# A spectral mixer and a gated feed-forward on one core: how slab 0 is loaded, where four statistics rows are kept, and how the last slab is gated

## The chip, the core and the metric

The kernel runs on one core of a Trainium2 chip. The metric is the device time of one launch in microseconds; the number given for a kernel is the median of several runs. Profiles are of one execution, with times in microseconds from the start of its span. The engines are TensorE (PE; its weight loads are listed as PEld), VectorE (DVE), ScalarE (ACT), GpSimd (POOL) and SyncE (SP), which here only issues transfers.

## What is computed

A layer norm over the rows of `x` (2048 by 640) feeds two branches, which are multiplied and added to `x`:

```python
xn = _layernorm(x, axis=-1)
s = irfft2(rfft2(xn) * (w_r + 1j * w_i))          # over both axes, to bf16
g = silu((gelu(xn @ w_gate) * (xn @ w_up)) @ w_down)
return x + s * g
```

`w_gate` and `w_up` are 640 by 1536, `w_down` is 1536 by 640. Inputs, weights and output are bf16.

## The kernel before

The 2048 rows are taken as 16 slabs of 128 rows (row = 16 * n2 + n1, slab n1), each a tile of 128 partitions by 640. Both branches run through TensorE. The spectral branch is a chain of matrix products with tables (`fold`, `spectral`, `inverse`), with transfers to DRAM and back between its stages, and its result is the tile `y`. The feed-forward branch goes by four groups of four slabs: `gate_up` makes twelve tiles `uT` of a group (lines 868 to 920), and `down` multiplies them with `Wd` and finishes one slab (lines 932 to 1008).

No engine's order is written out by hand. Every piece of work is a task with an engine, a modelled cost, a rank and the tasks and buffers that it depends on (`add`, line 128). `Plan.run` (line 159) plays a list schedule with these costs and emits the instructions in the order that comes out; a load has either a modelled transfer time or, with `land=`, a fixed due time in nanoseconds. Each engine then works through its own queue in order. So a change of a cost, a due time or a buffer can change the order of tasks far away from it.

At the start, TensorE runs seven products on constants (`keep_warm`, line 377) while the first loads are on their way. Slab 0 of `x` is issued on ACT's DMA queue (line 349), slabs 1 and up and the weights on SP's (from line 372). For slabs 0 to 3, `turn_raw` (line 452) transposes the raw slab on TensorE in five pieces of 128 columns into PSUM (line 461), and a copy (`copy_on`, line 296) puts them into `XR`. The first two tiles of `gate_up` are made from `XR`, not yet normalised ("early", line 872); they are corrected later on VectorE with the mean and the inverse deviation of each row, spread over all partitions in `RB` (lines 916 and 918). These rows come from the statistics in `RM`: a transpose (line 560), a copy to a work tile `th` (line 562), a store of 4 KB to the DRAM scratch `D5` (line 563) and a load of `D5` into all partitions of `RB` (line 564). The work tiles tagged `th` have two buffers; the statistics on ACT (lines 416 and 419) and the tanh of `down` use the same tag.

At the end, the last slab (15) is done in three parts of 256, 256 and 128 columns (line 941). For each part twelve products (line 966) fill a PSUM tile, ACT takes tanh of half of it (line 975), and VectorE makes `G2 = (tanh + 1) * ps` (line 980), which is twice the silu; the factor of a half sits in the tables of the spectral branch. `finish` then multiplies by `y` (line 948), adds `x` (line 953) and stores. The third part goes another way: VectorE multiplies `y` with the PSUM tile beside the tanh (line 986, `early`), then applies `(tanh + 1)` (line 989, `late`), adds `x` (line 995), and the store is issued on ACT's queue (line 998).

Of the kernel before, what the change touches and what calls it, by code (L numbers as in the profile page):

```python
# [15 lines left out]
P = 128  # L16
# [206 lines left out]
def kernel(  # L223
# [125 lines left out]
    nc.scalar.dma_start(out=X[:, 0, :], in_=xv[:, 0, :])  # L349
# [21 lines left out]
    x_in[0] = add(lambda e: None, "SP", (1, 1), (0, -5), size=1, land=3620)  # L371
    load_x(1, 2, land=4150)
    load_w(Wg, gv, g_in, 0, 2, land=5210)
    load_x(2, 3, land=5700)
    load_w(Wu, uv, u_in, 0, 2, land=6760)
    load_x(3, 4, land=7250)
# [75 lines left out]
    def turn_raw(n1):  # L452
        pt = Slot("sp")

        def half():
            return pt.tile[:, 0, :].bitcast(BF16)[:, 0:D]

        def mm(e):
            place(pt, (2, 512))
            for c in range(5):  # L460
                nc.tensor.transpose(out=half()[:, c * P:c * P + P], in_=X[:, n1, c * P:c * P + P], identity=ident)  # L461
        a = add(mm, "PE", c_pe(*[140] * 5), (0, n1), after=[x_in[n1], warmed], new=[pt], use=[sX])
        raw[n1] = add(lambda e: copy_on(e, XR[:, :, n1 * P + (n1 > 0):(n1 + 1) * P + (n1 > 0)], half().rearrange("p (c n) -> p c n", c=5)),
                      {"ACT": c_act(640)} if n1 < 1 else {"ACT": c_act(640), "DVE": (415, 560)}, None, (0, n1), after=[a], use=[pt], hold={0: 1000, 1: 1000}.get(n1, 200))
# [92 lines left out]
    sr, rt = Slot("sp"), Slot("th")  # L557
# [4 lines left out]
    t = add(lambda e: nc.vector.tensor_copy(out=place(rt, (P,), FP32)[0:8, :], in_=sr.tile[0:8, 0, 0:P]), "DVE", c_dve(128, 1, True), (0, 3.5), after=[t], new=[rt], use=[sr])  # L562
    rs = dma(D5, lambda: rt.tile[0:8, :], (0, -5, 0), 4096, after=[t], use=[rt])
# [368 lines left out]
    def down(n1):  # L932
# [11 lines left out]
        def finish(lo, hi, done, rank, first):  # L944
            def f1(e):
                if first:
                    place(yg, (D,))
                (nc.gpsimd if n1 in () else nc.vector).tensor_tensor(out=yg.tile[:, lo:hi], in0=y.tile[:, n1 % 2, lo:hi], in1=G2.tile[:, lo:hi], op=ALU.mult)
# [10 lines left out]
        for lo, hi, tag in parts:  # L959
# [24 lines left out]
            def early(e, lo=lo, hi=hi, ps=ps, yp=yp):  # L984
                place(yp, (hi - lo,), FP32)
                nc.vector.tensor_tensor(out=yp.tile, in0=y.tile[:, n1 % 2, lo:hi], in1=ps.tile[:, 0:hi - lo], op=ALU.mult)
# [62 lines left out]
```

## Time and profile before

| | |
|---|---|
| median of 5 runs | 203.12 us (202.22 to 203.31) |
| the profiled execution | 202.22 us |
| its span | 200.4 us |
| granted TensorE clock | 0.999 |
| matmuls | 1526 |
| HBM read, written | 22.51 MB, 9.19 MB |

The profiled execution is the fastest of the five, and its span is what the profile's times are counted in. Busy times are of instructions on an engine; matmuls are pipelined with modelled ends, so a busy TensorE isn't the same as one at its peak. In a line of the timeline the numbers are the start and the length in us, then engine, line, operation, output <- input, shape and count; in brackets stands the idle time of the engine just before, and what ended it. A transfer's bracket or wait names the load that was waited for. "PEq", "ACTq" and the like are the engines' queues, where transfers are issued.

### The profile page before, as it was taken

Reading aid. Unit: us, or ns where it says so; the run is one execution under the profiler, and the core shown is the slowest. Engines: PE = TensorE matmul, PEld = TensorE weight load, DVE = VectorE, ACT = ScalarE, POOL = GpSimd, SP = SyncE. Lnnn points to the kernel's source line nnn. Section 1 sums busy time; section 2 is a strip of 40 time slices with the busy share of each in tenths; the row PEclk is TensorE's granted clock in tenths of the full one; section 3 lists DMA queues with packets and bytes.
Section 4 is the critical chain, followed back from the end, with each engine's and each line's share of the span. In section 5 each row is a group of like instructions: output and inputs, shape, how many; then the busy total and the mean of one; then the engine's idle time right before and its main releaser. Section 6 shows DMA issues by size and latency. Waiting matters only on the chain.

```text
span 200.4 us, 4122 instructions
## 1 busy us (share of the span) xinstructions
PE 195.2 (97%) x1526; PEld 117.8 (59%) x1526; DVE 148.8 (74%) x321; ACT 126.9 (63%) x224; POOL 31.6 (16%) x71
## 2 busy tenths in 40 slices
PE   8999999999999999999999999999999999999991
PEld 3994444676544555777755455467755555457781
DVE  1898889997333159999998999933257789787774
ACT  3999969966432767777775667243466665675421
POOL 2604250697000000000000000000004022211210
PEclk9999999999999999999999999999999999999999
DMA  6999999898539676533234110117604243332432
GB/s 180 327 316 326 337 395 212 219 253 163 183 106 377 225 189 179 134 110 112 64 111 136 65 65 0 69 65 237 286 3 144 89 134 108 101 101 85 131 103 65
DMA packets 35894, 32.62 MB, mean 163 GB/s; under 512 B 10910, under 2 KB 32930, under 8 KB 35874
## 3 DMA queue, kind: packets, MB, share of 16 engines
q1 hardware_dynamic: 34434, 29.49, 49.8%
q0 software_dynamic: 1152, 2.66, 4.8%
q8 instruction: 12, 0.20, 0.4%
q10 hardware_dynamic: 288, 0.20, 0.3%
q14 instruction: 8, 0.07, 0.1%
HBM read 22.51 MB, written 9.19 MB: 158 GB/s over the span
## 4 chain that ended last, share of the span: by engine, by line
PE 96%; DMA 2%; ACT 0%; DVE 0%; issue 0%; DVEq 0%
PE pg L882 26%; PE pu L882 26%; PE pg L966 13%; PE pu L966 13%; PE sp L693 3%; PE sp L826 3%; PE sp L768 2%; PE sp L802 2%; PE sp L666 2%; PE sp L528 2%; DMA X<-in_A_x_dram 2%; PE sp L686 1%; PE sp L820 1%; PE sp L461 1%; PE sp L474 1%; PE sp L649 0%
## 5 line engine op out<-in xcount | busy, mean ns | idle before, releaser
L882 PE MATMUL pg<-xnT,Wg 128*128 128x512 bf16 (+1 forms) x245 | 57.4, 366 | 0.0
L882 PE MATMUL pu<-xnT,Wu 128*128 128x512 bf16 (+1 forms) x245 | 57.3, 366 | 0.0
L903 DVE TENSOR_TENSOR uT<-pu,ge 128x512 bf16<-128x512 f32 x46 | 31.7, 690 | 20.0 <-PE pu L882 14.5
L966 PEld LDWEIGHTS <-uT 128*128 128x128 bf16 x396 | 37.8, 98 | 13.5
L899 ACT ACTIVATE ge<-pg 128x512 bf16<-128x512 f32 x46 | 27.5, 599 | 23.1 <-PE pg L882 22.6
L882 PEld LDWEIGHTS <-Wg 128*128 128x128 bf16 x285 | 25.3, 98 | 22.5 <-issue 0.4
L882 PEld LDWEIGHTS <-Wu 128*128 128x128 bf16 x285 | 24.9, 98 | 21.7
L966 PE MATMUL pg<-Wd,uT 128*128 128x320 bf16 (+2 forms) x204 | 30.7, 293 | 0.0
L966 PE MATMUL pu<-Wd,uT 128*128 128x320 bf16 (+1 forms) x192 | 29.7, 297 | 0.0
L296 ACT CAST ma<-sp 128x644 bf16<-128x644 f32 (+1 forms) x32 | 23.4, 794 | 9.7 <-PE sp L826 7.9
L928 POOL COPY xr<-s 1x1 bf16<-1x1 bf16 x1 | 0.2, 179 | 100.7 <-DVE s L852 100.7
L296 ACT CAST mc<-sp 128x640 bf16<-128x640 f32 x16 | 10.8, 697 | 5.5 <-DMA D<-mc 4.8
L975 ACT ACTIVATE th<-pu 128x320 f32<-128x320 f32 (+1 forms) x16 | 7.0, 437 | 11.0 <-PE pu L966 9.6
L929 POOL DMA_DIRECT2D xr<-in_A_x_dram x16 | 8.8, 550 | 32.3 <-DVE res L953 30.2
L980 DVE SCALAR_TENSOR_TENSOR G<-th,pg 128x320 bf16<-128x320 f32 (+1 forms) x16 | 7.7, 482 | 8.3 <-ACT th L975 8.1
L296 ACT CAST IU<-sp 128x640 bf16<-128x640 f32 x16 | 10.9, 691 | 4.1 <-PE sp L768 4.1
L296 ACT CAST Vt<-sp 128x640 bf16<-128x640 f32 x16 | 10.8, 691 | 3.7 <-PE sp L802 3.7
L975 ACT ACTIVATE th<-pg 128x320 f32<-128x320 f32 (+2 forms) x17 | 7.3, 430 | 8.2 <-PE pg L966 8.0
L980 DVE SCALAR_TENSOR_TENSOR G<-th,pu 128x320 bf16<-128x320 f32 (+1 forms) x16 | 7.7, 482 | 5.6 <-ACT th L975 5.3
L844 DVE TENSOR_TENSOR mb<-ma 128x640 bf16<-128x640 bf16 x8 | 3.9, 492 | 6.9 <-ACT ma L296 6.9
L409 DVE BATCH_NORM_STATS2 STAT<-X 128x6 f32<-128x320 bf16 x12 | 5.5, 484 | 4.0 <-DMA X<-in_A_x_dram 4.0
L746 DVE TENSOR_TENSOR R<-Y 64x644 bf16<-64x644 bf16 x16 | 7.8, 490 | 0.4
(104 smaller groups left out, 254.5 us busy)
## 6 DMA issues: line engine op xcount, KB each, us to landing
BU<-D SPq DMA_DIRECT2D x8, 640.0 KB
D<-mc SPq DMA_DIRECT2D x8, 320.0 KB
D<-IU SPq DMA_DIRECT2D x8, 320.0 KB
xr<-in_A_x_dram POOLq DMA_DIRECT2D x16, 160.0 KB, 2.6
out_dram<-res SPq DMA_DIRECT2D x15, 160.0 KB
Wg<-in_B_w_gate_dram SPq DMA_DIRECT2D x6, 320.0 KB
Wu<-in_B_w_up_dram SPq DMA_DIRECT2D x6, 320.0 KB
Wd<-in_B_w_down_dram SPq DMA_DIRECT2D x6, 320.0 KB
```

The source lines that it names most:

```text
L296: return nc.scalar.copy(out=out, in_=in_) if e == "ACT" else nc.vector.tensor_copy(out=out, in_=in_)
L409: nc.vector.bn_stats(out=STAT[:, n1, 6 * g:6 * g + 6], in_=x[:, 320 * g:320 * g + 320])
L693: nc.tensor.matmul(into(q, ri), lhsT=sZ.tile[:, q, ri, :], rhs=FM[:, kinds[q][2] + (4 if ri and kind == 0 else 0), :], start=False, stop=T ...
L746: nc.vector.tensor_tensor(out=o, in0=Yf[:, ::-3, :], in1=Yf[:, 1:3, :], op=ALU.subtract)
L826: nc.tensor.matmul(into(q, s), lhsT=svs[s].tile[:, c, :], rhs=IM[:, q, :], start=False, stop=True, skip_group_check=True)
L882: nc.tensor.matmul(ps.tile[:, lo:hi + more], lhsT=w[:, c, t * P:(t + 1) * P], rhs=XR[:, c, lo + (lo > 0):hi + 1 if lo or more else hi] if ...
L899: nc.scalar.activation(out=ge.tile, in_=pg.tile if src is None else src, func=ACT.Gelu_apprx_tanh)
L903: nc.vector.tensor_tensor(out=u.tile, in0=pu.tile if src is None else src, in1=ge.tile, op=ALU.mult)
L929: nc.gpsimd.dma_start(out=sx.tile, in_=xv[:, n1, :])
L966: nc.tensor.matmul(ps.tile[:, 0:hi - lo], lhsT=uT[grp, ks[i]].tile[:, j * P:(j + 1) * P], rhs=Wd[:, ks[i], lo:hi], start=(i == 0), stop=(i ...
L975: nc.scalar.activation(out=th.tile[:, 0:hi - lo], in_=ps.tile[:, 0:hi - lo], func=ACT.Tanh, scale=0.5)
L980: nc.vector.scalar_tensor_tensor(out=G2.tile[:, lo:hi], in0=th.tile[:, 0:hi - lo], scalar=1.0, in1=ps.tile[:, 0:hi - lo], op0=ALU.add, op1 ...
```

## The change

Four things are edited. Slab 0 is loaded by SP's queue as the first of its loads instead of by ACT's queue, and the due times of the loads are set anew. The transposes of slab 0 go in two steps of three and two pieces, into the two halves of the PSUM tile, each with a copy of its own on ACT. The statistics rows are copied into eight partitions of `RB` itself rather than into a `th` tile, and stored from there. For slab 15, ACT applies Silu in place of tanh, straight into `G2`, for all three parts; `finish` multiplies by `y` and by 2.0 in one VectorE instruction, and the third part goes through `finish` as well, with its store on ACT's queue as before. The modelled cost of the first Silu has 1300 ns added.

```diff
-    nc.scalar.dma_start(out=X[:, 0, :], in_=xv[:, 0, :])
...
-    x_in[0] = add(lambda e: None, "SP", (1, 1), (0, -5), size=1, land=3620)
-    load_x(1, 2, land=4150)
-    load_w(Wg, gv, g_in, 0, 2, land=5210)
-    load_x(2, 3, land=5700)
-    load_w(Wu, uv, u_in, 0, 2, land=6760)
-    load_x(3, 4, land=7250)
+    load_x(0, 1, land=3600)
+    load_x(1, 2, land=4050)
+    load_w(Wg, gv, g_in, 0, 2, land=5110)
+    load_x(2, 3, land=5600)
+    load_w(Wu, uv, u_in, 0, 2, land=6660)
+    load_x(3, 4, land=7150)
...
+        parts = ((0, 3), (3, 5)) if n1 < 1 else ((0, 5),)
+        for k, (lo, hi) in enumerate(parts):
+            def mm(e, k=k, lo=lo, hi=hi):
+                if k == 0:
+                    place(pt, (2, 512))
+                for c in range(lo, hi):
+                    nc.tensor.transpose(out=half(k)[:, c * P:c * P + P], in_=X[:, n1, c * P:c * P + P], identity=ident)
+
+            def cp(e, k=k, lo=lo, hi=hi):
+                copy_on(e, XR[:, lo:hi, n1 * P + (n1 > 0):(n1 + 1) * P + (n1 > 0)], half(k)[:, lo * P:hi * P].rearrange("p (c n) -> p c n", c=hi - lo))
...
-    t = add(lambda e: nc.vector.tensor_copy(out=place(rt, (P,), FP32)[0:8, :], in_=sr.tile[0:8, 0, 0:P]), "DVE", c_dve(128, 1, True), (0, 3.5), after=[t], new=[rt], use=[sr])
-    rs = dma(D5, lambda: rt.tile[0:8, :], (0, -5, 0), 4096, after=[t], use=[rt])
+    t = add(lambda e: nc.vector.tensor_copy(out=RB[0:8, 0, 0, :], in_=sr.tile[0:8, 0, 0:P]), "DVE", c_dve(128, 1, True), (0, 3.5), after=[t], use=[sr])
+    rs = dma(D5, RB[0:8, 0, 0, :], (0, -5, 0), 4096, after=[t])
...
+                if last:
+                    nc.vector.scalar_tensor_tensor(out=yg.tile[:, lo:hi], in0=y.tile[:, n1 % 2, lo:hi], scalar=2.0, in1=G2.tile[:, lo:hi], op0=ALU.mult, op1=ALU.mult)
+                    return
...
+            if last and hi == D:
+                add(lambda e: nc.scalar.dma_start(out=outv[:, n1, lo:], in_=res.tile[:, lo:]), "ACT", (430, 430), (0, 0, n1), after=[t], use=[res], size=256 * (hi - lo))
+                return
...
+            def gate(e, lo=lo, hi=hi, ps=ps):
+                if lo == 0:
+                    place(G2, (D,))
+                nc.scalar.activation(out=G2.tile[:, lo:hi], in_=ps.tile[:, 0:hi - lo], func=ACT.Silu)
+            if last:
+                a = add(gate, "ACT", c_act(hi - lo, extra=0 if lo else 1300), (0, step[0]), after=mm[-1:] + done, new=[] if lo else [G2], use=[ps, G2] if lo else [ps])
+                done.append(a)
+                finish(lo, hi, [a], (0, step[0]), lo == 0)
+                continue
```

With these go the lines of `early`, `late` and the branch for the third part (984 to 1002 before).

## The prediction, made before the changed kernel had run

> **What bounds the kernel now.** I read the page's totals first, then the windows, then TensorE's waits, the chain, and the timeline of both ends. The totals and the chain say TensorE:
>
> ```profile
> span 200.4 us, 4122 instructions
> PE 195.2 (97%) x1526; PEld 117.8 (59%) x1526; DVE 148.8 (74%) x321; ACT 126.9 (63%) x224; POOL 31.6 (16%) x71
> PE 96%; DMA 2%; ACT 0%; DVE 0%; issue 0%; DVEq 0%
> ```
>
> A busy share is an average, so the next two views ask where the missing 5.2 us lie: busy time by window, and everything that TensorE waited for.
>
> ```profile
> 4.00:8.00 4.00, 3.67 (x53) 3.51 (x54) 3.48 (x15) 3.17 (x6) 1.57 (x4) 1.00 1.08 311
> 8.00:12.00 4.00, 4.00 (x75) 4.00 (x73) 3.55 (x11) 3.55 (x8) 1.52 (x5) 1.00 1.13 332
> 196.00:200.40 4.40, 0.37 (x7) 0.20 (x4) 1.56 (x7) 0.40 (x2) 0.00 (x0) 0.95 0.23 74
> ...
> PE sp L367 <- PEq L1033: 0.8, 1, 0.8
> PE pg L882 <- ACT XR L296: 0.2, 1, 0.2
> PE sp L461 <- DMA X<-in_A_x_dram: 0.2, 1, 0.2
> ```
>
> The columns of a window are its length, then the busy time of PE, its loads, DVE, ACT and POOL. From 8 to 196 us PE is full in every window I asked for; it waits three times in all, and all three lie before 5.6 us. Its work is fixed, so the end moves by three things only: when the first product starts, what runs after the last product, and any new hole between. The first end:
>
> ```profile
> 4.08 1.25 PE L461 MATMUL sp<-ident,X 128*128 128x128 bf16 x10 [0.17 <-DMA X<-in_A_x_dram]
> 4.83 1.29 ACT L296 COPY XR<-sp 128x640 bf16<-128x640 bf16 x2 [2.17 <-PE sp L461]
> 5.57 0.73 PE L882 MATMUL pg<-XR,Wg 128*128 128x129 bf16 x10 [0.25 <-ACT XR L296]
> 7.41 0.49 DVE L409 BATCH_NORM_STATS2 STAT<-X 128x6 f32<-128x320 bf16 x1 [0.25 <-DMA X<-in_A_x_dram]
> 7.56 0.44 PE L461 MATMUL sp<-ident,X 128*128 128x128 bf16 x5
> ```
>
> Slab 0 lands at 4.03 (in the chain its DMA runs 0.72 to 4.03), five transposes and one copy follow, and the products start at 5.57. Slab 3 lands at about 7.4, where DVE waits for it, and PE reaches it at 7.56 without a wait: a lead of only 0.15. The other end:
>
> ```profile
> 195.74 0.39 ACT L975 ACTIVATE th<-pu 128x256 f32<-128x256 f32 x1 [0.93 <-PE pu L966]
> 196.41 0.28 ACT L975 ACTIVATE th<-pg 128x128 f32<-128x128 f32 x1 [0.28 <-PE pg L966]
> 196.72 0.29 DVE L986 TENSOR_TENSOR mc<-s,pg 128x128 f32<-128x128 bf16 x1
> 196.93 0.28 DVE L948 TENSOR_TENSOR yg<-s,G 128x256 bf16<-128x256 bf16 x1
> 197.13 0.28 DVE L989 SCALAR_TENSOR_TENSOR yg<-th,mc 128x128 bf16<-128x128 f32 x1
> 197.33 0.29 DVE L953 TENSOR_TENSOR res<-yg,xr 128x256 bf16<-128x256 bf16 x1
> 197.53 0.22 DVE L995 TENSOR_TENSOR res<-yg,xr 128x128 bf16<-128x128 bf16 x1
> 197.78 0.36 ACTq L998 DMA_DIRECT2D out_dram<-res  x1
> ```
>
> PE is done at 196.4. VectorE then works off five operations, two of them left over from the second part, and the last store leaves at 197.78; from there to the end is 2.62 us of transfer and closing.
>
> **What the Trainium skill says.** On the table: "ScalarE: Activation LUTs", What ACT_TABLE_LOAD costs, prices a switch of function set at 1283 ns of load plus about 1380 ns of drain. The trace agrees with the first (its one load takes 1.28 us); with the drain it doesn't visibly agree: the next ACTIVATE starts at 2.46, 0.02 after the load's end at 2.44. "ScalarE activation tables: per-element evaluation and per-set limits", What a function is on this engine, says that a function costs the same whichever table is read; so I give Silu the durations of tanh. No page says whether Silu shares a set with gelu and tanh. "DMA: Bandwidth & Descriptors", Issuing engines are not separate DMA queues, says that loads issued from several engines interleave on the same 16 DMA engines and only issue time is saved. The trace fits: from 2.6 us they move some 350 GB/s, and the share stays at 1.0 or more to 8 us.
>
> **The change, part by part.**
>
> *Slab 0 on SP.* Now slabs 0 and 1 are issued together at 0.72 on two queues and share the engines. Summing the windows of 0.2 us, the stream starts at 2.4, and the 0.33 MB of both have moved by 3.4; slab 0 lands 0.63 later, at 4.03. Alone in front, its 0.164 MB have moved by 2.92 and land at about 3.55. PE's seven warming products hold it to about 3.77 (0.76 + 7 x 0.43), so the transposes start there instead of at 4.08: 0.31 earlier. Every SP issue behind it comes one issue later, about 0.46 us (slab 1 from 0.72 to 1.18, Wg to 1.64, slab 3 from 2.68 to about 3.2). I cost that at nothing: slab 1 can begin at 2.4 + 0.46 = 2.86, just as slab 0 ends, and after that the transfers, not the issues, set the pace (slab 3's bytes move near 6 us). Without that cover it costs up to 0.46. On ACT's queue the 0.41 us issue ahead of the table load goes, which nobody waits for.
>
> *Two copies instead of one.* The transposes run 0.107 apart, so the third ends 0.21 before the fifth. A copy of 640 takes 0.70; at 0.83 ns per element (tanh: 0.28 at 128, 0.38 at 256) 384 take 0.49 and 256 take 0.38, and back-to-back copies overlap by 0.10. From the third transpose to the end: 0.04 + 0.49 - 0.10 + 0.38 = 0.81, against 0.21 + 0.04 + 0.70 = 0.95 now. Gain 0.14; ACT is charged 0.07 more. The first product can start at 5.57 - 0.31 - 0.14 = 5.12. The first columns of Wg allow that, barely: 0.656 MB have moved by 4.32, landing about 4.95.
>
> The 0.45 doesn't all last. The loads are no faster in sum, so slab 3 still lands near 7.4, and PE in its fixed order would reach it at 7.1 and wait. If it lands as now, only 0.10 is left (7.46 instead of 7.56); if it lands 0.1 earlier, as the due times in the diff assume, 0.20; if the new order puts other products ahead of it, up to 0.45. I take 0.25.
>
> *Rows in a corner of RB.* The same copy (0.27) and the same 4 KB store (issued at 17.04) as now. RB is filled only by the load that follows that store, so no wait is added. A "th" buffer comes free earlier, perhaps letting slab 7's statistics (L416, 20.54) run sooner on an ACT that is 85% busy there; PE isn't waiting: 0. The cover is PE's backlog; without it a late RB costs what it is late.
>
> *Silu and the gate.* For the last part go L986, L989 and their place in DVE's queue; for the first two, L980 (0.42 each). New: Silu in place of tanh, three scalar_tensor_tensor, the same adds. The trace shows no such operation on bf16 from SBUF at 256 columns; it lies between 0.29 (tensor_tensor, L948) and 0.42 (L980 from PSUM). I take 0.42, and 0.28 for 128 columns (L989). A dependent DVE step starts 0.03 after its source ends (195.50 + 0.29 to 195.82). Second part: Silu ends 196.13, gate 196.16 to 196.58, add 196.61 to 196.90. Last part: Silu 196.41 to 196.69, gate at 196.81 behind that add's issue (0.20 step) to 197.09, add 197.12 to 197.34, store at 197.37: 0.41 earlier. With the cheap gate the last gate starts at 196.72 and the store leaves at 197.2: 0.55.
>
> The table: if Silu is in another set, one load of 1.28 is due between the tanh of slab 14 (193.12 to 193.56) and the first Silu (194.43). If it needn't wait for PE it ends at 194.84, and the first Silu is 0.41 late, before two parts with slack: nothing lost. If it stands behind the wait for PE, it ends at 195.71; queued behind it are all three Silus, the third still at 196.41, but DVE's six steps then start at 196.1 and end near 197.6, a gain of 0.15. I take 0.48 for this part, between 0.41 and 0.55.
>
> *Sum:* 0.25 + 0.48 = 0.73. On the profiled execution: span 199.7, time 201.5 (1.82 lies around its span, 202.22 - 200.4). That execution is 0.90 below the median 203.12; from the median I get **202.39 us**.
>
> **Rivals.**
> A. Both ends gain as above: 202.39, own range 201.9 to 202.9. For it: the three waits and the five DVE steps are all at the ends. Chance 0.50.
> B. The gain is mostly eaten: slab 3's landing leaves 0.10 and the table load waits, leaving 0.15: 202.9. For it: the lead of 0.15 at 7.41. Against it: only one of the two need fail. Chance 0.22.
> C. Slower, by the plan: all instructions are ordered by a planner from modelled costs, and new due times and tasks reorder everything after 4 us. The order now has no hole in 190 us; the new one need not be so lucky. Place: a PE product put ahead of a transfer or an evacuation that comes later than modelled, most likely from 8 to 50 us, where DVE, ACT and DMA are near full. One such wait costs what the late thing is late; it decides from 0.73 + 0.6 = 1.3 us, and at 1.6 gives 203.12 - 0.73 + 1.6 = 204.0. Against it: the order of before has held 0.00 of waits there. Chance 0.20.
> D. The switch of set costs load and drain, 2.66, behind the wait at 194.43: first Silu at 197.1, last ends near 198.0, store near 198.5, 0.7 later than now; with 0.10 in front, 203.7. It decides from about 1.4, where the third Silu would move. Against it: no drain after the load at 1.16. Chance 0.08.
>
> **How the numbers follow.** This kernel's runs can tell about 0.3% (0.6 us) from no change: faster means under 202.5, slower over 203.7. A gives faster 0.41 and same 0.09; B faster 0.06, same 0.16; C slower 0.17, same 0.03; D slower 0.05, same 0.03. Faster 0.47, same 0.31, slower 0.22. The range takes A's lower end (0.45 + 0.55, and 0.3 for the draw of the median) and reaches past B and D into C until about 0.15 is left above: 201.8 to 203.9.
>
> **What would show it.** Slab 0 landing at 3.5 to 3.6 and the first L882 near 5.1; then whether L461 for slab 3 shows a wait on the load of X. A second ACT_TABLE_LOAD after 193.5, and whether it starts before PE's part is done. The last store at 197.2 to 197.4 less the front's gain. PE's list of waits: any entry after 8 us is C. Wrong is the reasoning if slab 0 lands no earlier, or if PE waits in the middle.

## The result, and the profile after

The changed kernel takes **203.97 us** (median of 31 runs, 202.81 to 204.9). The kernel before, run beside it 52 times, takes 202.62 (202.18 to 204.31); the five runs shown above had a median of 203.12. The ratio is 1.0054, 95% interval [1.0043, 1.0066]: the change makes the kernel slower by half a per cent. (The ratios and intervals are those recorded with the runs; they aren't quotients of the two medians, which would be 1.0067 here.) The forecast was 202.39 and faster. It was counted from the median of the first five runs; from 202.62 the same gain of 0.73 would give 201.89. Each experiment below is compared with the kernel before on its own chip; the medians of before lie between 202.51 and 202.65 there.

The page of the changed kernel (its profiled execution took 204.92 us, which is 0.95 above the median), first its totals and then the shares of the chain that ended last:

```profile
span 203.2 us, 4119 instructions
PE 194.8 (96%) x1526; PEld 117.4 (58%) x1526; DVE 147.3 (73%) x318; ACT 127.5 (63%) x226; POOL 30.8 (15%) x71
...
PE 92%; DMA 4%; ACT 1%; issue 0%; SPq 0%; DVE 0%; DVEq 0%; ACTq 0%
```

TensorE has the same 1526 matmuls and no more busy time (194.8 against 195.2); the span is 2.7 longer (203.15 against 200.44, before rounding). So the loss lies in waits, and the list of everything that TensorE waited for says in which (the numbers are us in total, times, longest):

```profile
PE pg L889 <- DMA Wg<-in_B_w_gate_dram: 1.9, 1, 1.9
PE sp L535 <- ACT mc L296: 1.7, 2, 1.5
PE sp L366 <- PEq L1034: 0.8, 1, 0.8
```

The last was there before. The first two are new, one at the start and one in the middle. The timeline of the start:

```profile
0.72 0.86 SPq L303 DMA_DIRECT2D X<-in_A_x_dram  x2
1.63 0.43 SPq L303 DMA_DIRECT2D Wg<-in_B_w_gate_dram  x1
...
3.71 0.74 PE L463 MATMUL sp<-ident,X 128*128 128x128 bf16 x10
...
6.31 0.74 PE L889 MATMUL pg<-XR,Wg 128*128 128x129 bf16 x10 [1.87 <-DMA Wg<-in_B_w_gate_dram]
...
8.23 0.49 DVE L408 BATCH_NORM_STATS2 STAT<-X 128x6 f32<-128x320 bf16 x1 [0.31 <-DMA X<-in_A_x_dram]
8.35 0.44 PE L463 MATMUL sp<-ident,X 128*128 128x128 bf16 x5
```

The transposes do start 0.37 earlier than before (3.71 against 4.08), but the first product starts 0.74 later (6.31 against 5.57), since the first columns of `Wg` are late, and slab 3, on which VectorE waits until 8.23, lands 0.8 later (7.41 before). TensorE reaches slab 3 at 8.35 instead of 7.56: 0.79 lost. The middle, the lines of SP's queue, ACT and PE around the wait:

```profile
42.93 5.00 SPq L499 DMA_TRANSPOSE xnT<-s  x3
48.02 0.54 SPq L303 DMA_DIRECT2D D<-mc  x1
51.37 1.29 ACT L296 CAST mc<-sp 128x640 bf16<-128x640 f32 x2 [3.31 <-DMA D<-mc]
52.11 0.38 PE L535 MATMUL sp<-mb,F1T 128*128 128x512 bf16 x1 [1.54 <-ACT mc L296]
```

Three transposing transfers stand in SP's queue ahead of a store of an `mc` tile. They take 5.0 us where three such issues of 1.23 would take 3.7; the store leaves at 48.02, ACT waits 3.31 us for it before it can write the next `mc` (there are two buffers), and TensorE waits 1.70 for ACT's copies. The end:

```profile
196.38 1.28 ACT L999 ACT_TABLE_LOAD   x1
197.67 0.38 ACT L999 ACTIVATE G<-pg 128x256 bf16<-128x256 f32 x1
...
199.21 0.28 ACT L999 ACTIVATE G<-pg 128x128 bf16<-128x128 f32 x1 [0.28 <-PE pg L979]
...
200.18 0.37 ACTq L968 DMA_DIRECT2D out_dram<-res  x1
```

TensorE's last matmul ends at 199.17 (198.34 + 0.83), and the last store leaves 1.01 us after it; before it was 1.41 (196.37 to 197.78). The end gains 0.40 up to that store. But the way from the last store to the end of the span is 0.30 longer (2.97 against 2.67, before rounding), so little of the gain is left. That isn't chance: it is 2.96 to 2.97 in all five profiles of kernels planned with the new due times, whichever queue loads slab 0, and 2.48 to 2.67 in the other fifteen. The last store lands 1.59 after its issue in both; a closing step on SP comes 0.33 later. Why isn't shown. So this execution's 2.7 us come from 0.79 at the start and 1.70 in the middle, less 0.40, plus 0.30 at the end; 0.3 are not located.

### The profile page after: what moved, and what is told of

Read it like the earlier page. It is cut to its first block, busy times and chain, and to the rows that moved or that the text cites. A ratio compares the mean times of both kernels' runs of the same rounds, so it can differ in the third digit from the quotient of the medians.

```text
span 203.2 us, 4119 instructions
## 1 busy us (share of the span) xinstructions
PE 194.8 (96%) x1526; PEld 117.4 (58%) x1526; DVE 147.3 (73%) x318; ACT 127.5 (63%) x226; POOL 30.8 (15%) x71
## 4 chain that ended last, share of the span: by engine, by line
PE 92%; DMA 4%; ACT 1%; issue 0%; SPq 0%; DVE 0%; DVEq 0%; ACTq 0%
PE pg L889 26%; PE pu L889 26%; PE pu L979 12%; PE pg L979 12%; PE sp L700 3%; PE sp L833 3%; PE sp L775 2%; DMA Wg<-in_B_w_gate_dram 2%; PE sp L809 2%; PE sp L673 2%; DMA D<-mc 2%; PE sp L535 1%; PE sp L693 1%; PE sp L827 1%; PE sp L481 1%
## 5 line engine op out<-in xcount | busy, mean ns | idle before, releaser
L906 ACT ACTIVATE ge<-pg 128x512 bf16<-128x512 f32 x46 | 28.0, 609 | 25.4 <-PE pg L889 25.3
L993 DVE SCALAR_TENSOR_TENSOR G<-th,pg 128x320 bf16<-128x320 f32 x15 | 7.3, 488 | 10.2 <-ACT th L988 9.9
L988 ACT ACTIVATE th<-pg 128x320 f32<-128x320 f32 x15 | 6.6, 440 | 10.4 <-PE pg L979 10.2
L993 DVE SCALAR_TENSOR_TENSOR G<-th,pu 128x320 bf16<-128x320 f32 x15 | 7.3, 487 | 6.1 <-ACT th L988 6.0
L988 ACT ACTIVATE th<-pu 128x320 f32<-128x320 f32 x15 | 6.7, 444 | 7.8 <-PE pu L979 6.6
L296 ACT CAST Z<-sp 128x1024 bf16<-128x1024 f32 x8 | 7.9, 1016 | 2.5 <-PE sp L673 2.5
L415 ACT ACTIVATE th<-X 128x640 bf16<-128x640 bf16 x10 | 7.7, 785 | 1.2 <-DMA X<-in_A_x_dram 1.2
```

Of the source, the lines that this page charges most:

```text
L296: return nc.scalar.copy(out=out, in_=in_) if e == "ACT" else nc.vector.tensor_copy(out=out, in_=in_)
L415: nc.scalar.activation(out=place(junk, (D,)), in_=x, func=ACT.Copy, scale=-1.0 / D, accum_out=less)
L906: nc.scalar.activation(out=ge.tile, in_=pg.tile if src is None else src, func=ACT.Gelu_apprx_tanh)
L988: nc.scalar.activation(out=th.tile[:, 0:hi - lo], in_=ps.tile[:, 0:hi - lo], func=ACT.Tanh, scale=0.5)
L993: nc.vector.scalar_tensor_tensor(out=G2.tile[:, lo:hi], in0=th.tile[:, 0:hi - lo], scalar=1.0, in1=ps.tile[:, 0:hi - lo], op0=ALU.add, op1 ...
```

## The experiments

Theory 1 after the result: moving slab 0 to SP's queue costs at the start, the new order costs in the middle, and the Silu gate gains what was forecast (up to the last store). Rivals: the table load or Silu costs more than it brings; the statistics rows in `RB` cost; the middle's wait follows from the transfers at the start and not from the order.

### The parts alone

**Silu alone**: `down` of the changed kernel in the kernel before; TensorE's order doesn't move (in short form).

```diff
-            th = tanh(...) ; G2 = (th + 1) * ps ; early / late for the third part
+            nc.scalar.activation(out=G2.tile[:, lo:hi], in_=ps.tile[:, 0:hi - lo], func=ACT.Silu)
+            finish(lo, hi, [a], (0, step[0]), lo == 0)
```

> Only the gate of slab 15 is changed; TensorE's order is that of before and slab 0 stays on ACT's queue. Theory 1 (the tail does what the forecast said, and what it saved in the changed kernel was lost behind its last store because that store was the first on ACT's queue): last store 0.4 us earlier after TensorE's end than before, 2.6 us from it to the end of the span, time 0.4 us less than before (ratio 0.998). Theory 2 (the table load or the extra ACT work costs something by itself): last store earlier but time the same or more. Theory 3 (the saved 0.4 is lost in the store whatever was on the queue earlier): 3.0 us from the store to the end, ratio 1.000.

Measured: 202.22, ratio 0.998 [0.9965, 0.9995]. Its timeline at the end:

```profile
193.65 1.28 ACT L992 ACT_TABLE_LOAD   x1
194.95 0.38 ACT L992 ACTIVATE G<-pg 128x256 bf16<-128x256 f32 x1
...
197.46 0.35 ACTq L961 DMA_DIRECT2D out_dram<-res  x1
```

The load stands directly before the first Silu and ends 0.02 ahead of it. The last store leaves 1.01 after TensorE's end (195.62 + 0.83), as in the changed kernel, and 0.32 earlier than before (197.78); 2.67 follow, as before. The end gains 0.2%. The expectation blamed the longer way behind the last store on that store being the first on ACT's queue; with slab 0 moved and nothing else (the next kernel) it is the first too, and the way is 2.51.

**Slab 0 on SP, nothing else**: one word of line 349; due times and the orders of all engines stay.

```diff
-    nc.scalar.dma_start(out=X[:, 0, :], in_=xv[:, 0, :])
+    nc.sync.dma_start(out=X[:, 0, :], in_=xv[:, 0, :])
```

> Only the issue of slab 0 moves from ACT's queue to the head of SP's; every engine's order stays that of before. Theory 1 (SP's issues for the weights come 0.46 us later while the first slabs start 0.4 us sooner, so the stream has a hole and all that follows lands later): slab 0 lands near 3.0, the first columns of Wg near 6.2, slab 3 near 8.2; TensorE reaches slab 3 about 0.8 us later than the 7.56 of before; time +0.6 to +0.9 us (ratio 1.003 to 1.0045). Theory 2 (the forecast: a stream without a hole): slab 3 lands at 7.4 and the time is 0.1 to 0.4 us less. Theory 3 (the new due times and the order made from them delay it): with the old order kept, no change at all.

Measured: 203.01, ratio 1.003 [1.0015, 1.0045]. The loss at the start needs nothing but the queue. TensorE's timeline:

```profile
5.66 1.26 PE L882 MATMUL pg<-XR,Wg 128*128 128x129 bf16 x10 [0.69 <-DMA Wg<-in_B_w_gate_dram]
...
7.25 1.27 PE L882 MATMUL pg<-XR,Wg 128*128 128x128 bf16 x10
```

Here is more than the wait of 0.69. Ten products of 128 columns take 1.27 us, and the next instruction starts 1.07 after them; before, ten took 0.73 and the next started 0.57 after (6.42 to 6.99). TensorE runs at half pace until 9.6 us in this execution (203.91 us, one of the slower ones; five of the 22 lie above 203.8).

**The rows in RB alone** (in short form):

```diff
-    ... out=place(rt, (P,), FP32)[0:8, :] ... ; rs = dma(D5, lambda: rt.tile[0:8, :], ...)
+    ... out=RB[0:8, 0, 0, :] ... ; rs = dma(D5, RB[0:8, 0, 0, :], (0, -5, 0), 4096, after=[t])
```

> Only the rows in a corner of RB instead of a th tile. TensorE's order becomes that of the changed kernel but for two products. Theory 1 (the freed th buffer reorders the plan, and this order has the wait for a copy of ma near 52 us behind the stores from mc): a TensorE wait on the mc copy of 0.5 to 1.8 us between 45 and 55 us, time +0.5 to +1.7 us (ratio 1.0025 to 1.008), with more spread than before. Theory 2 (the wait in the middle follows from the late loads at the start): no wait, time the same as before. Theory 3 (the forecast: the edit is free): the same time.

Measured: 202.39, ratio 0.9986 [0.9975, 0.9997]. TensorE's order becomes that of the changed kernel but for two products near 30 us, it has no wait in the middle, and it isn't slower. On SP's queue the `mc` store stays ahead of the third transposing transfer (44.39 and 45.02), as before.

**The split of slab 0's transposes alone** (the two-step loop of the change in `turn_raw`, the rest as before):

```diff
+        parts = ((0, 3), (3, 5)) if n1 < 1 else ((0, 5),)
```

> Only the two-step transposes and copies of slab 0; TensorE's order is that of before. Forecast: the first product starts 0.14 us earlier, and at most 0.10 of it is left behind slab 3: time 0 to 0.14 less, not told from no change (ratio 0.9993 to 1.000). Rival: the extra ACT instruction (0.07) pushes ACT, which is full from 5 to 10 us, and TensorE gains waits on XR: time +0.1 to +0.3.

Measured: 202.51, ratio 0.9991 [0.9975, 1.0007], not told from no change. The first product starts at 5.27 instead of 5.57; 0.09 of this is that the transposes began earlier in that execution (3.99 against 4.08), so the split brings 0.21.

**The loads alone**: slab 0 on SP with the new due times, so that the plan is made anew.

```diff
-    x_in[0] = add(lambda e: None, "SP", (1, 1), (0, -5), size=1, land=3620)
+    load_x(0, 1, land=3600)
```

> Only slab 0 on SP and the new due times, so the order is planned anew; gate, split and rows as before. With the old order this load cost 0.3%. Theory 1 (the due times, 0.1 us earlier while the loads really land 0.4 to 0.8 us later, make an order with waits): ratio 1.005 or more and waits of TensorE after 8 us. Theory 2 (the wait near 52 us needs the RB edit together with these due times): the same as with the old order, ratio 1.003, and no wait in the middle.

Measured: 203.19, ratio 1.0038 [1.0019, 1.0058], not told from the one-word edit. TensorE has no wait in the middle, and two transposing transfers, not three, stand ahead of the `mc` store on SP's queue. In the profiled execution (204.98 us) TensorE is at half pace until 10.2.

**All but the load**: the changed kernel with slab 0 on ACT's queue and the old due times; made twice, in two batches.

```diff
+    nc.scalar.dma_start(out=X[:, 0, :], in_=xv[:, 0, :])
-    load_x(0, 1, land=3600)
+    x_in[0] = add(lambda e: None, "SP", (1, 1), (0, -5), size=1, land=3620)
```

> The changed kernel with slab 0 back on ACT's queue and the old due times; the split, the rows in RB and the Silu gate stay. Theory 1 (the load on SP with its due times is the whole loss, at the start and through the order it makes): no wait of TensorE after 6 us, and the three gains add: ratio 0.998 x 0.9986 x 0.9991 = 0.9957, about 0.9 us less than before. Theory 2 (the edits hurt each other whatever the load does): a wait in the middle and a ratio over 0.999.

> The same as all_but_sp, whose interval (0.9967 to 1.0017) left open whether the three gains add. If they do, 0.9957 to 0.997; if not, 0.998 to 1.001 and a wait of TensorE that the other parts alone don't have.

Measured: 202.53, ratio 0.9992 [0.9967, 1.0017], and 202.31, ratio 0.9981 [0.9965, 0.9997]. The other three parts together are worth up to 0.2% (the first interval includes no gain), and the load with what it does to the plan turns that into a loss of 0.5%. The three single ratios would multiply to 0.9957: the gains don't add in full. In both profiles the `mc` store goes out ahead of the third transposing transfer. So the order of the changed kernel, with that store behind it, arises, in these runs, only when the new due times meet another of the edits.

**Silu and RB**: the two edits above in the kernel before.

> Before with the Silu gate and the rows in RB, and neither the load on SP nor the split. If the two gains (ratios 0.998 and 0.9986) add: 0.9966, about 0.7 us less than before. If all_but_sp's 0.9992 was right and the parts hurt each other: 0.998 to 1.000.

Measured: 202.17, ratio 0.9993 [0.9976, 1.0009]. The product of the two single ratios would be 0.9966, below that interval. In its profile TensorE waits 0.9 for the `mc` copies in the middle. Here the store (44.45) stands ahead of the held transposing transfer (45.07, 2.19 us), yet ACT can write the next `mc` only at 49.66, 5.2 us after the store's issue; in nine other profiles of this place it is 3.2 to 4.6. So the middle can wait for a store without the load on SP and without the order of the changed kernel. Why this store took so long isn't shown.

### The middle: the order or the early transfer?

**The changed kernel again**, as the control of its batch.

> The changed kernel once more, for a second trace beside the others. If the wait near 52 us belongs to its order, it is there again, with 0.5 to 1.8 us; if it was an accident of the first profile, TensorE waits only at the start, and the time of that profiled run is near 203.0. Ratio 1.003 to 1.007.

Measured: 203.93, ratio 1.0039 [1.0017, 1.0062]. The waits are 1.4 at the start and 1.2 in the middle; the third of the transposing transfers, issued at 44.48, is held 2.91, and the store leaves at 47.49.

**The changed kernel's orders with slab 0's transfer issued from ACT's queue**; due times and the order of every other instruction as in the changed kernel.

```diff
+    nc.scalar.dma_start(out=X[:, 0, :], in_=xv[:, 0, :])
-    load_x(0, 1, land=3600)
+    x_in[0] = add(lambda e: None, "SP", (430, 430), (0, -4, seq[0]), use=[sX], size=163840, land=3600)
```

> The changed kernel with every engine's order kept, and only slab 0's transfer issued from ACT's queue instead of SP's. Theory 1 (the hole at the start costs 0.6 to 0.9 us, the order in the middle costs the rest): slab 3 lands near 7.4 again, but a TensorE wait on the mc copy near 50 us stays; ratio about 0.999 to 1.002, and 0.6 to 0.9 us less than the changed kernel. Theory 2 (the wait in the middle is only the late start carried on): no wait after 6 us, ratio 0.996.

Measured: 202.72, ratio 1.0004 [0.9988, 1.0021]. SP's queue in the middle:

```profile
40.89 3.88 SPq L501 DMA_TRANSPOSE xnT<-s  x3
44.86 1.04 SPq L303 DMA_DIRECT2D D<-mc  x1
```

The same three transfers in the same order take 3.88. The third goes out at 43.54 and isn't held; in the two profiles of the changed kernel it goes out at 45.59 and 44.48, held 2.34 and 2.91. TensorE has no wait there. So this one edit of the changed kernel takes away its loss against before (1.0039 in the same batch), at the start and in the middle. The order alone isn't enough, then; it makes the place where a delay can do harm.

**The changed kernel with the store first**: one swap in SP's order, the third transposing transfer behind the store of `mc`. The orders of PE, ACT and DVE stay.

```diff
-        for t in plan.run():
+        line = plan.run()
+        at = line.index(stored[4])
+        back = [i for i in range(at) if line[i] in turns][-1]
+        line.insert(at, line.pop(back))
+        for t in line:
```

> The changed kernel with one swap on SP's queue: the fifth store from mc goes ahead of the transposing transfer that stood before it (issued at 44.48 and held for 2.91 us in the last trace); TensorE, VectorE and ACT keep their orders. Theory 1 (the wait in the middle is this store held behind that transfer, and the mc copy held behind the store): the store leaves near 45 instead of 47.5, ACT's wait for it falls from 2.8 to about 1 us, TensorE no longer waits on the mc copy near 51, and the time falls by about 1 us, to a ratio of 1.000 to 1.002. Theory 2 (the DMA engines are busy with the transposes then and the store would be as late anyway): TensorE's wait stays at 1 us or more, ratio 1.004 to 1.006.

Measured: 202.81, ratio 1.0022 [1.0005, 1.004]. The timeline of SP and ACT:

```profile
44.38 0.53 SPq L303 DMA_DIRECT2D D<-mc  x1
45.01 3.20 SPq L499 DMA_TRANSPOSE xnT<-s  x2
48.35 1.29 ACT L296 CAST mc<-sp 128x640 bf16<-128x640 f32 x2 [0.74 <-DMA D<-mc]
```

The transfer is held again, 45.01 onwards, but the store is out before it. ACT waits 0.74 instead of 3.31 and TensorE not at all; its list of waits shows only the two of the start:

```profile
PE sp L366 <- PEq L1040: 0.8, 1, 0.8
PE pg L889 <- DMA Wg<-in_B_w_gate_dram: 0.6, 1, 0.6
```

The swap takes the ratio from 1.0054 (1.0039 in the second batch) to 1.0022, in another batch: the middle costs some 0.2 to 0.3%, though the interval of the second batch alone overlaps. By the medians (203.97 and 203.93 to 202.81) it would be 1.1 us. That the wait is gone with the swap is shown by the list; its exact worth isn't, since this execution's wait for `Wg` is shorter too (0.6 against 1.9 and 1.4). What holds a transposing transfer issued near 45 us isn't shown; one issued at 44.81, in the kernel with the split alone, took 1.26. It is held in the kernel before too, where the store stands ahead of it:

```profile
43.20 1.22 SPq L492 DMA_TRANSPOSE xnT<-s  x1
44.51 0.53 SPq L303 DMA_DIRECT2D D<-mc  x1
45.10 1.82 SPq L492 DMA_TRANSPOSE xnT<-s  x1
```

### The start: why Wg is late, and what that costs

The windows of 0.4 us (columns: PE, loads, DVE, ACT, POOL, granted clock, DMA share, GB/s), with one of 1.2 us ahead of them, first of the kernel before, then of the changed one:

```profile
1.60:2.80 1.20, 1.20 (x4) 0.41 (x3) 0.00 (x0) 1.05 (x2) 0.24 (x4) 1.00 0.72 144
2.80:3.20 0.40, 0.40 (x2) 0.15 (x1) 0.00 (x0) 0.00 (x0) 0.00 (x0) 1.00 1.04 368
3.20:3.60 0.40, 0.40 (x2) 0.00 (x0) 0.00 (x0) 0.00 (x0) 0.00 (x0) 1.00 1.14 350
3.60:4.00 0.40, 0.31 (x1) 0.00 (x0) 0.00 (x0) 0.00 (x0) 0.00 (x0) 1.00 1.17 344
```

```profile
1.60:2.80 1.20, 1.20 (x4) 0.41 (x3) 0.00 (x0) 0.61 (x2) 0.24 (x4) 1.00 0.79 221
2.80:3.20 0.40, 0.40 (x2) 0.15 (x1) 0.19 (x1) 0.00 (x0) 0.00 (x0) 1.00 0.73 209
3.20:3.60 0.40, 0.40 (x2) 0.15 (x1) 0.40 (x2) 0.00 (x0) 0.00 (x0) 1.00 0.57 117
3.60:4.00 0.40, 0.40 (x6) 0.29 (x5) 0.36 (x2) 0.00 (x0) 0.00 (x0) 1.00 0.75 209
```

With both slabs on one queue in front, the stream has a hole from 2.8 to 4.0: (368 + 350 + 344 - 209 - 117 - 209) x 0.4 = 211 KB fewer moved. But it also picks up earlier, and (221 - 144) x 1.2 = 92 KB more have moved by 2.8. What is left behind at 4.0 is 119 KB, 0.34 us at 350 GB/s. Both slabs are there by 3.7 (ten transposes run through). The packet records of the two traces tell slabs and weights apart, since a row of a slab is a packet of 1280 bytes and a piece of `Wg` or `Wu` one of 512. The 256 packets of slabs 0 and 1 have started by 3.20 (before: 3.49). Packets of 512 bytes begin at 2.84, 1.2 us after `Wg` is issued, but slowly: 43, 89 and 163 start in the three windows from 2.8 to 4.0, against 30, 228 and 264 before. The 640 that the first columns of `Wg` make up have started by 5.01 instead of 4.43. So the hole is the slow beginning of `Wg` with nothing else to fill it. It makes about 0.6 us; that `Wg` is there only at 6.31, and why its packets begin so slowly, isn't explained by this. It varies, too: with the same issue time TensorE's wait for `Wg` ends between 5.56 and 6.49 in seven profiles. Three kernels with slab 0 on SP, otherwise in the order of before, try to mend it.

**The first columns of Wg from ACT's queue**, at 0.72:

```diff
+    nc.scalar.dma_start(out=Wg[:, :, 0:2 * P], in_=gv[:, :, 0:2 * P])
```

> Slab 0 on SP's queue, and the first columns of Wg on ACT's queue at 0.72 in its place; all orders of before. Theory 1 (the hole is there because the first Wg load, issued at 1.6, begins to move only 2 us after its issue): with Wg issued at 0.72 it moves from about 2.7, no hole before 4 us, Wg lands by 4.5, slab 0 at 3.0 to 4.0, slab 3 near 7.4, TensorE does not wait for Wg; ratio 0.998 to 1.000. Theory 2 (two queues share, and slab 0 waits for Wg's bytes in its stead): no hole, but slab 0 and 1 land near 4.5 and the time is that of before or 0.2 us more.

Measured: 202.67, ratio 1.0021 [1.0004, 1.0038]. The hole is gone (285, 348 and 383 GB/s in the three windows) and no wait for `Wg` is left, but TensorE now waits 0.76 for slab 1, and the profiled execution (204.01 us) is at half pace until 9.4.

**Slab 0, Wg, slab 1** on SP's queue:

```diff
-    load_x(1, 2, land=4150)
     load_w(Wg, gv, g_in, 0, 2, land=5210)
+    load_x(1, 2, land=4150)
```

> Slab 0 on SP's queue, then the first Wg load, then slab 1: Wg is issued at 1.18 as in the kernel before; every engine's order is that of before. Theory 1 (a Wg load begins to move only 2 us after its issue, so it must be issued by 1.2): Wg moves from about 3.2, lands near 5.0 as before, TensorE does not wait for it; slab 1 lands behind it, before 5.5; a short hole from 2.6 to 3.2 stays; ratio 0.999 to 1.001. Theory 2 (a single queue makes the hole whatever the order): Wg lands at 5.6 or later, TensorE waits 0.6 us or more, ratio 1.003.

Measured: 202.97, ratio 1.0025 [1.0007, 1.0042]. TensorE's timeline:

```profile
3.71 0.74 PE L461 MATMUL sp<-ident,X 128*128 128x128 bf16 x5
4.81 0.72 PE L461 MATMUL sp<-ident,X 128*128 128x128 bf16 x5 [0.36 <-DMA X<-in_A_x_dram]
5.32 1.26 PE L882 MATMUL pg<-XR,Wg 128*128 128x129 bf16 x10
```

The hole is nearly closed up to 4.4 (274 to 378 GB/s from 2.8 to 4.0), but another follows: 101 to 233 GB/s from 4.6 to 5.4. The first product starts 0.25 earlier than before, and this execution takes 202.26. Yet the median isn't better. Its 22 times show why: fourteen lie between 202.26 and 203.0, eight between 203.38 and 204.19. Since `Wg` isn't late here, a late `Wg` can't be all that slab 0 on SP costs.

**Ten warming products instead of seven**:

```diff
-            for k in range(n):
+            for k in range(n + 3):
```

> Slab 0 on SP in the order of before (ratio 1.003 with seven warming products), with ten warming products in place of seven, so that TensorE stays at work until slab 0's transposes at about 5.0 and hardly pauses for Wg. Theory 1 (part of the loss is that TensorE's pause at 5 us keeps its clock at half speed for some us more in a part of the runs): the steps are short from 6 us in the profile, runs over 203.8 us become rare (six of 22 before), and the median falls or stays, ratio 1.000 to 1.003. Theory 2 (only the late landing counts): the same tail of slow runs, ratio 1.003 or more, since the first product starts near 5.9.

Measured: 202.98, ratio 1.0026 [1.0011, 1.004]; the first product starts at 6.47, and four of 22 runs lie above 203.35. TensorE has no pause before 5.9 us then, but the first product starts 0.9 later than before because the transposes wait for the warming products, and the loss stays what it was; this run tells little.

Counted over all batches, with a line drawn afterwards at 203.35, 20 of 328 runs of the kernel before lie above it, and 8 of 122 in the seven experiments above with slab 0 on ACT's queue; of the six with slab 0 on SP other than the changed kernel itself it is 37 of 132. Three profiled executions of that upper group (203.91, 204.01 and 204.98) show TensorE at half pace until 9.4 to 10.2 us, while in the kernel before ten products take 0.57 from step to step by 6.4. The Trainium skill, "TensorE: Matmul & The Clock Gate", Part 1: The HAM clock gate, says that the array starts at half its clock and goes to full after a window of about 3.4 us of sustained work, that the windows run freely, whatever the kernel does, and that the step from one 128-column product to the next is 106.7 ns at the low clock and 55.6 at the full one. The two steps agree with the trace (1.07 and 0.57 for ten). That the rise isn't tied to the kernel's start shows as well: in the profiles without a pause of 0.4 us or more before it, full pace comes anywhere from 3.8 (the changed kernel's own profile, 3.0 us after the first matmul and so sooner than one such window) to 6.7 (the rows in `RB` alone). That gives theory P: TensorE's pause before its clock has risen (0.69 with slab 0 on SP, against 0.17 and 0.25 in the kernel before) spoils such a window in some executions, which then stay at half pace for another. Rival S: the upper group belongs to slab 0 in front of SP's loads, through some transfer, and not to the pause.

The four runs that tell these apart leave out the transposition of slabs 4 to 15: plain transfers of the same size take the place of the twelve transposing ones, in the same order, so the times are those of another result.

```diff
-nc.sync.dma_start_transpose(out=xnT[:, :, n1 * P:(n1 + 1) * P], in_=sxn.tile[:, n1 % 2, :])
+nc.sync.dma_start(out=xnT[:, :, n1 * P:(n1 + 1) * P], in_=sxn.tile[:, n1 % 2, :].rearrange("p (c n) -> p c n", c=5))
```

**The base**: this edit alone, the order of before.

> The order of the kernel before, with the twelve transposing transfers of slabs 4 to 15 replaced by plain transfers of the same size to the same place; the transposition of these slabs is left out. The base of this batch. Its median may lie some tenths from that of the kernel before; both theories expect at most a tenth of its runs 1 us or more above its own median, as for the kernel before.

Measured: 202.71 (14 runs, 202.25 to 203.41), ratio 0.9994 [0.9974, 1.0015] to the kernel before. The base stands in for it well.

**A pause without touching a transfer**: five warming products instead of seven.

```diff
-            for k in range(n):
+            for k in range(n - 2):
```

> The base of this batch (transposition of slabs 4 to 15 left out) with five warming products instead of seven; all transfers and orders as in the base. PE then stands still from about 2.9 to 4.08 us, 1.2 us, before its clock has risen. Theory P (a pause of PE before its clock has risen keeps it at half pace for some microseconds more, whichever queue loads slab 0): a quarter or more of the runs lie 1 us or more above the base's median, or the whole kernel moves up by that; the profile shows products 107 ns apart until 9 us or later. Rival S (the slower group comes with slab 0 in front of SP's loads and not with the pause): median within 0.2 of the base's and no more of a slower group than there.

Measured: 203.67 (202.93 to 204.4), ratio 1.0046 [1.0029, 1.0063]. The whole kernel moves up by 1.0 us. TensorE's timeline, first of the base and then of this kernel:

```profile
4.06 1.25 PE L461 MATMUL sp<-ident,X 128*128 128x128 bf16 x10 [0.15 <-DMA X<-in_A_x_dram]
5.55 0.73 PE L882 MATMUL pg<-XR,Wg 128*128 128x129 bf16 x10 [0.25 <-ACT XR L296]
```

```profile
4.06 1.25 PE L461 MATMUL sp<-ident,X 128*128 128x128 bf16 x10 [1.00 <-DMA X<-in_A_x_dram]
5.55 1.24 PE L882 MATMUL pg<-XR,Wg 128*128 128x129 bf16 x10 [0.25 <-ACT XR L296]
...
7.12 1.27 PE L882 MATMUL pg<-XR,Wg 128*128 128x128 bf16 x10
8.19 0.99 PE L882 MATMUL pu<-XR,Wu 128*128 128x129 bf16 x10
```

The first product starts at 5.55 as in the base, no product waits for a load after that, and still the work is at half pace until about 8.8. The window from 8.0 to 9.2, of the base and then of this kernel, with matmuls counted in the brackets behind PE's busy time:

```profile
8.00:9.20 1.20, 1.20 (x25) 1.20 (x23) 1.06 (x5) 1.20 (x4) 0.77 (x3) 1.00 1.13 334
```

```profile
8.00:9.20 1.20, 1.20 (x18) 1.20 (x17) 0.24 (x2) 0.88 (x3) 0.70 (x3) 1.00 1.16 328
```

18 matmuls instead of 25 in the same 1.2 us of a fully busy TensorE; the granted clock is given as 1.00 in both. Busy time and the clock column don't show the half pace, only the counts and steps do.

**Slab 0 on SP**, on this base:

> The base of this batch (transposition of slabs 4 to 15 left out) with slab 0 on SP's queue, orders as in the base: sp_slab0_same_order with plain transfers. Both theories: 0.3 to 0.5 above the base's median, a quarter to a third of the runs 1 us or more above it.

Measured: 203.1 (202.08 to 204.44), ratio 1.0031 [1.0012, 1.005]; eight of 22 runs at 204.11 to 204.44, none between them and 203.25. The cost is that of the one-word edit, without any transposing transfer. The pause doesn't cost in every execution. The profiled one (202.47) is among the fast:

```profile
3.70 1.27 PE L461 MATMUL sp<-ident,X 128*128 128x128 bf16 x10
5.92 0.74 PE L882 MATMUL pg<-XR,Wg 128*128 128x129 bf16 x10 [0.95 <-DMA Wg<-in_B_w_gate_dram]
```

TensorE is at half pace before the pause of 0.95 and at full pace behind it.

**Slab 0 on SP with the pause filled**: slab 1's transposes three times, to the same place, which keeps TensorE busy while it would wait for `Wg`.

```diff
-            for c in range(5):
+            for c in list(range(5)) * (3 if n1 == 1 else 1):
```

> The same as pl_slab0_sp (transposition of slabs 4 to 15 left out), with the five transposes of slab 1 on PE made three times over, the same result to the same place, so that PE is busy in its wait for Wg from about 4.9 us on. Theory P: at most a tenth of the runs 1 us or more above the base's median; the rest up to 0.3 above those of pl_slab0_sp, since ten products at half pace outlast the wait of 0.7 by 0.4. Rival S: a quarter to a third of the runs in the slower group, as in pl_slab0_sp, and the median no lower than there.

Measured: 202.59 (202.36 to 203.45), ratio 0.9992 [0.9979, 1.0004], and none of 14 runs in the group above 204. TensorE's timeline of one execution (203.45, the slowest of the 14):

```profile
3.71 2.34 PE L461 MATMUL sp<-ident,X 128*128 128x128 bf16 x20
6.49 0.74 PE L882 MATMUL pg<-XR,Wg 128*128 128x129 bf16 x10 [0.45 <-DMA Wg<-in_B_w_gate_dram]
```

Ten matmuls that compute nothing new make the kernel 0.5 us faster than it is without them. In this execution `Wg` is late (the first product starts at 6.49), but the clock has risen; that it is the slowest of the 14 fits the first product being 0.94 later than in the base. When `Wg` lands in the faster ones isn't known. Rival S falls on both sides: the pause alone brings a loss, and filling it takes the loss away with slab 0 still on SP. Both are shown on the base without transposing transfers, whose times stand in for those of the kernel itself.

## Why the prediction was wrong, step by step

- **What bounds the kernel: right.** The profile shows the end moved by the first product, the tail and new holes. Two things it took as fixed moved too: the pace of TensorE at the start, and the way behind the last store.
- **"The transposes start there instead of at 4.08: 0.31 earlier": right** (0.37), since the warming products hold them as it said. Slab 0 itself was there at 3.0 (VectorE starts on it at 3.01), 0.5 before the 3.55 of the forecast: the stream picks up earlier with it in front, and the 2.4 was carried over from the kernel before.
- **"I cost that at nothing": this is the step that failed.** Its cover was that "slab 1 can begin at 2.4 + 0.46 = 2.86, just as slab 0 ends, and after that the transfers, not the issues, set the pace". The second half fails: the stream runs half dry from 2.8 to 4.0, where that of before, on two queues, ran full at 344 to 368 GB/s. `Wg` costs TensorE a wait of 1.87. The price named without cover, up to 0.46, was too small as well: 0.79 at slab 3 in the profile, while the later packets of `Wg` explain about 0.6. The prediction used what the Trainium skill, "DMA: Bandwidth & Descriptors", Issuing engines are not separate DMA queues, says: that issuing from several engines saves only issue time. Its cover was that the transfers then set the pace, and in the trace of the changed kernel they don't from 2.8 to 4.0. Its reading that the share stays at 1.0 or more up to 8 us was too round even for the kernel before: from 4.6 to 5.4 it is 0.81 to 0.96, at 234 to 291 GB/s.
- **The other missing term is TensorE's clock.** The prediction valued a wait in front at its length. A pause before the clock has risen can cost about 1.0 us more (a pause of 1.0 with the first product no later: the median 0.96 above its base). Filling the pause brings the load's 1.0031 down to 0.9992 [0.9979, 1.0004], against 0.9994 of the base, so on that base this term is most of the load's cost. How the two share in the changed kernel itself, whose two profiles show the clock up in time and a wait for `Wg` of 1.9 and 1.4 instead, stays open.
- **Split: 0.14 forecast.** Alone it brings the first product forward by 0.21 from the start of the transposes, and by ratio nothing that can be told from no change. In the changed kernel `Wg` ends last, so it brings nothing.
- **Rows in RB: "0" was about right for the part.** No wait was added by the rows, and alone they gave 0.9986. That the edits together can give an order that none of them gives alone has no term: three transposing transfers ahead of the `mc` store stand only in the changed kernel.
- **Rival C named this**: a TensorE product ahead of a late evacuation, price 1.6, chance 0.20. It came at 51 to 52 us with 1.70 in the profile, and at 0.2 to 0.3% by the store's swap. But C is only a part of the loss, and its total of 204.0, close to the 203.97 measured, is partly luck: it counts from a median 0.5 too high and keeps a gain of 0.73 that didn't come. The evidence against it, that the order of before had no such wait, was given too much weight: the same transfer was held 1.82 us there, with the store ahead of it by the planner's order.
- **Silu and the gate: 0.48 forecast (0.41 to 0.55), 0.40 measured** from TensorE's end to the last store, 0.2% alone. In the changed kernel 0.30 of it is lost behind the last store, a stretch that the forecast held fixed at 2.62. The price taken for the new VectorE step, 0.42, is right (0.43). The table load of 1.28 isn't held by the wait for TensorE; the first Silu is 0.48 late at 197.67 (its products end at 197.19), forecast 0.41, and the slack of two parts hides it. Rival D falls: no drain shows behind the load.

The parts multiply to 0.9981 (all but the load, its second batch) x 1.003 (the load) x about 1.002 to 1.003 (the store behind the transfers) = 1.003 to 1.004, against 1.0054 [1.0043, 1.0066]. The longer way behind the last store, 0.3 us or 0.15%, is of the size of the rest, but no run tests it. Three versions are faster than the kernel before by their intervals: Silu alone, 0.998 [0.9965, 0.9995], the rows in `RB` alone, 0.9986 [0.9975, 0.9997], and all but the load, 0.9981 [0.9965, 0.9997], though its first batch gave 0.9992 [0.9967, 1.0017].

## What to carry to other kernels

In the first microseconds count what the transfer engines move in each short window, before moving a load from one queue to another: here two queues in front kept the stream full where one left a hole. Keep TensorE busy without a pause until its clock has risen, with idle products if they don't delay the work (ten warming products did; the repeated transposes, going by the median, didn't), and look for that in the step between matmuls, since busy time and the clock column don't show it. Where a planner orders the queue, look in the profile of before for transfers that are already held and ask what would stand behind them in another order. And look at the stretch behind the last store, which moved here by as much as the gain.

## What the runs showed of the hardware that was not expected

- A pause of TensorE of 1.0 us at 3 to 4 us cost 0.96 us of median, although the first product started no later (5.55); ten useless transposes in the pause near 5 us gained 0.5 us. A pause of 0.95 cost no half pace afterwards in one profiled execution.
- Full pace came at a different time from one execution to the next: 3.8 to 6.7 us without a long pause, 8.8 to 10.2 in four profiles with a pause of 0.69 to 1.00.
- At half pace a fully busy TensorE did 18 matmuls in 1.2 us instead of 25, and the granted clock read 1.00.
- A transposing transfer takes 1.23 us of SP's queue; issued near 45 us it took 1.26 to 2.91 in these kernels, and what stood behind it waited.
- The load of the Silu table (1.28 us) runs as soon as ACT is free, ahead of the wait for the data, and the first Silu starts 0.01 to 0.02 us after it.
